# Sink tables on other engines, an output between two units, and two gate halves ahead of their val halves in a fused attention and SwiGLU kernel

## The chip, the cores and the metric

The kernel runs on one core of one Trainium2 chip. The metric is the device time of one execution in microseconds (us); for the kernel before the change four executions are given, and their median is 241.62 us. A change of 1% is 2.42 us. In the profile PE is TensorE's matmuls and PEld its weight loads, DVE is VectorE, ACT is ScalarE, POOL is GpSimd, SP is SyncE.

## What is computed

Windowed attention with four sink keys, then a SwiGLU block on its output (cut):

```python
# q, k, v: (4, 8, 768, 64); n_sink 4, window 128; x: 3072 tokens of 512
scores = scale * np.matmul(q, k.transpose(0, 1, 3, 2))
is_sink = pos[None, :] < int(n_sink)
rel = pos[:, None] - pos[None, :]
in_window = (rel >= 0) & (rel < int(window))
scores = np.where(is_sink | in_window, scores, -1000000000.0)
a = np.exp(scores - np.max(scores, axis=-1, keepdims=True))
a = a / (np.sum(a, axis=-1, keepdims=True) + 1e-09)
x = np.matmul(a, v).transpose(0, 2, 1, 3).reshape(B * S, H * D)
g = x @ w_gate                       # 512 x 1536
silu = g * (1.0 / (1.0 + np.exp(-g)))
val = x @ w_val                      # 512 x 1536
out = silu * val @ w_out             # 1536 x 512
```

## The kernel before

Everything is one hand-written order: each engine gets its instructions in the order in which the code issues them, and semaphores join the engines.

The 3072 tokens are cut in two ways. Attention works on 12 groups of 256 tokens (three for each of the four batches). The SwiGLU block works on eight token blocks of 256, 256, 256, 512, 512, 512, 512 and 256 tokens; block 0 is group 0, block 1 is group 1, block 2 is group 2, block 3 is groups 3 and 4, and so on.

For a group, `step_T` or `step_TN` transposes keys and queries on TensorE, or `xbar` lets SP's DMA queue do it from the tile `nat`. `step_S` makes the scores, ACT takes their exponential into `e`, and DVE multiplies by the window mask (L313). `step_K` multiplies the queries with the batch's sink keys, which `step_ks` has copied into `kss` (L274). `step_PV` starts from the sink values, which `step_vsb` has spread into the block-diagonal table `vsb` (L279), adds the window values, and then normalises into `xn`: DVE takes the reciprocal (L372) and either DVE multiplies (L378, put off until the next `flush`) or, with `norm="a"`, ACT does (L375). `step_X` turns `xn` into `xT`, the input of the block: by TensorE transposes for groups 0, 1, 2 and 4 (L402, evicted by ACT at L405 or by DVE at L409), by a DMA transpose on SP's queue for the others (L397).

A block is worked in units. A gate unit (`gate`) projects 512 columns with `w_gate` into the PSUM bank `pg` (eight matmuls of 256 columns, or four of 512), ACT takes `th`, then come the attention steps that are woven into the unit, then the projection with `w_val` into `pv`; DVE makes `u` from `th` and `pg` (L445) and `ht` from `u` and `pv` (L446). A down unit (`down`) multiplies `ht` with `w_out` for 128 tokens into `pd` (L463), ACT copies it out, and SP's queue issues the output DMA (L471). `weave` runs a list of units, each with the attention steps of its slot. The units of the first list are gate units 0, 1 and 2 of block 0 (columns f=0, 2, 4), then 0, 1 and 2 of block 1, then the rest of both; `wg`, `wv` come in six pieces of two column chunks, and unit f=4 needs the third piece, `wg2` and `wv2`. Both halves of a unit use PSUM banks from one ring of eight.

POOL issues all loads of q, k, v and the weights in one order. The order ends, before the first matmuls, with `load_nat(2)`, `load_gate(3)`, `load_v(2)`, `load_gate(4)`, `load_gate(5)` and the four pieces of `w_out`. There are eight semaphores for these loads, used in turn, so that a load waits until the eighth before it has landed. `nat` from group 4 on has one buffer: a load of the next group waits for the transposes of the last.

Of the kernel before, what the change touches and what calls it, by code (L numbers as in the profile page):

```python
# [7 lines left out]
FP32 = mybir.dt.float32  # L8
BF16 = mybir.dt.bfloat16
AF = mybir.ActivationFunctionType  # L10
ALU = mybir.AluOpType
# [3 lines left out]
def kernel(  # L15
# [12 lines left out]
    nc = tc.nc  # L28
    P = 128
# [7 lines left out]
    DMC = DM // P  # L37
# [4 lines left out]
    SIZES = [256, 256, 256, 512, 512, 512, 512, 256]  # L42
# [6 lines left out]
    FOF = [(i, f - sum(FCH[:i])) for i in range(len(FCH))  # L49
           for f in range(sum(FCH[:i]), sum(FCH[:i + 1]))]  # L50
# [27 lines left out]
    def bank(shape, dtype, name):  # L78
        return psum.tile(shape, dtype, tag="b", name=name)
# [24 lines left out]
    def load_nat(g):  # L104
        b, c = divmod(g, GC)
        x = (natp if g > 3 else rowp).tile(
            [P, 2, 2, DM], BF16, tag="nat" if g > 3 else "rows", name="nat")
        for i, src in ((0, k), (1, q)):
            for j in range(2):
                t0 = c * 256 + j * P  # L110
                nc.gpsimd.dma_start(  # L111
                    x[:, i, j].rearrange("p (h d) -> p h d", d=D),
                    src[b, :, t0:t0 + P].rearrange("h p d -> p h d"))
        nats[g] = x

    def load_v(g):
        b, c = divmod(g, GC)
        va = vpool.tile([P, 2, H, VS], BF16, tag=f"va{g}", name="va")
        nc.vector.memset(va[:, :, :, D:D + 1], 1.0)
        for j in range(2):  # L120
            t0 = c * 256 + j * P
            nc.gpsimd.dma_start(  # L122
                va[:, j, :, 0:D], v[b, :, t0:t0 + P].rearrange("h p d -> p h d"))
        vas[g] = va

    wgs, wvs, wos = [], [], []

    def load_gate(i, which=(0, 1)):
        f0, n = sum(FCH[:i]) * P, FCH[i] * P
        both = (wgs, moe_w_gate, "wg"), (wvs, moe_w_val, "wv")  # L130
        for lst, w, nm in (both[x] for x in which):
            t = wpool.tile([P, DMC, n], BF16, tag=f"{nm}{i}", name=nm)
            nc.gpsimd.dma_start(
                t, w[:, f0:f0 + n].rearrange("(c p) f -> p c f", p=P))
            lst.append(t)

    def load_out(i):
        n = DFC // 4
        t = wpool.tile([P, n, DM], BF16, tag=f"wo{i}", name="wo")
        nc.gpsimd.dma_start(  # L140
            t, moe_w_out[i * n * P:(i + 1) * n * P].rearrange("(c p) f -> p c f", p=P))
        wos.append(t)
# [57 lines left out]
    load_gate(1, (1,))  # L200
    load_gate(2)
    nc.gpsimd.tensor_copy(out=vcf[64:128], in_=vcf[0:64])
    load_nat(2)
    load_gate(3)
    load_v(2)
    load_gate(4)
    load_gate(5)
    for i in range(4):
        load_out(i)

    nc.vector.tensor_scalar(ident, tq, tk, None, op0=ALU.is_equal)
    tq2 = tq.rearrange("p (o x) -> p o x", o=1).broadcast_to([P, 2, P])
# [3 lines left out]
    kTs, qTs, es_t, e_t, xns, xTs = {}, {}, {}, {}, {}, {}  # L216
    later = []

    def flush():
        for f in later:  # L220
            f()
        later.clear()

    def new_T(b):
        if b not in kTs:
            kTs[b] = kqtp.tile([P, NP2, S], BF16, tag="kT", name="kT")
            qTs[b] = kqtp.tile([P, NP2, S], BF16, tag="qT", name="qT")

    def step_T(g, i, p2, evict=None):
        b, c = divmod(g, GC)  # L230
        new_T(b)
        x = rows[g]
        pt = bank([P, 2, 256], FP32, "pt")
        for pp in range(2):
            p = 2 * p2 + pp
            for r in range(4):
                for w in range(2):
                    h = slice(64 * w, 64 * (w + 1))
                    nc.tensor.matmul(
                        pt[h, pp, r:256:4], x[h, i, p, r * D:(r + 1) * D],  # L240
                        ident[h, h], start=True, stop=True, skip_group_check=True)
        dst = (kTs, qTs)[i][b][:, 2 * p2:2 * p2 + 2, c * 256:(c + 1) * 256]
        if (evict or ("a", "v")[i]) == "a":
            nc.scalar.copy(out=dst, in_=pt)
        else:
            nc.vector.tensor_copy(out=dst, in_=pt)
# [24 lines left out]
    def step_ks(b):  # L271
        for h in range(2):
            r = slice(h * D, (h + 1) * D)
            nc.vector.tensor_copy(  # L274
                out=kss[r, b, :, h * NS:(h + 1) * NS], in_=kTs[b][r, :, 0:NS])

    def step_vsb(b):
        vsb = const.tile([P, 4, D + 1], BF16, tag=f"vsb{b}", name="vsb")
        nc.vector.tensor_tensor(  # L279
            vsb,  # L280
            (vcl[:, b - 1:b] if b else vcf).broadcast_to([P, 4, D + 1]),
            diag_h.rearrange("q (h o) -> q h o", o=1).broadcast_to([P, 4, D + 1]),
            op=ALU.mult)
        vsbs.append(vsb)
# [100 lines left out]
    def dense(t, c, n):  # L385
        return t[:, 0:c * n].rearrange("p (c n) -> p c n", c=c)
# [27 lines left out]

    hts = {}

    def gate(tb, f, attn):
        n = SIZES[tb]
        two = 512 // n
        if tb not in hts:  # L420
            t = hpool.tile([P, DFC * 512], BF16, tag="ht", name="ht")
            hts[tb] = dense(t, DFC, n)
            if tb == 0:
                hts[1] = t[:, DFC * n:2 * DFC * n].rearrange("p (c n) -> p c n", c=DFC)
        x = xTs[tb]

        def project(ws, name):
            ps = bank([P, 512], FP32, name)
            for i in range(two):
                fi, fo = FOF[f + i]  # L430
                for c in range(DMC):
                    nc.tensor.matmul(  # L432
                        ps[:, i * n:(i + 1) * n], ws[fi][:, c, fo * P:(fo + 1) * P],
                        x[:, c], start=(c == 0), stop=(c == DMC - 1))
            return ps

        pg = project(wgs, "pg")
        th = tpool.tile([P, 512], FP32, tag="th", name="th")
        nc.scalar.activation(th, pg, AF.Tanh, scale=0.5)  # L439
        for a in attn:  # L440
            a()
        pv = project(wvs, "pv")

        u = upool.tile([P, 512], BF16, tag="u", name="u")
        nc.vector.scalar_tensor_tensor(u, th, 1.0, pg, op0=ALU.add, op1=ALU.mult)  # L445
        nc.vector.tensor_tensor(  # L446
            hts[tb][:, f:f + two].rearrange("p a n -> p (a n)"), u, pv, op=ALU.mult)
        flush()

    def down(tb, ts, attn, last=False):  # L450
# [26 lines left out]
    def gates(tb):  # L477
        return [(gate, tb, f) for f in range(0, DFC, 512 // SIZES[tb])]
# [4 lines left out]
    def A(fn, *a):  # L483
        return lambda: fn(*a)

    def TN(g, evict="av"):
        return [A(step_TN, g, i, j, evict) for j in range(2) for i in range(2)]

    def Ss(g):
        return [A(step_S, g, p2) for p2 in range(2)]  # L490

    def PVs(g):
        return [A(step_PV, g, j, hh) for hh in range(2) for j in range(2)]

    def Xs(g):
        return [A(step_X, g, j) for j in range(2)]

    def K(g):
        return A(step_K, g)
# [84 lines left out]
    for p in range(1, NP2):  # L584
# [2 lines left out]
    nc.vector.scalar_tensor_tensor(lt8, th8, 0.0, lt8, op0=ALU.is_ge, op1=ALU.mult)  # L587
    nc.vector.tensor_reduce(diag_h, lt8.rearrange("p q h -> p h q"), mybir.AxisListType.X,
                            op=ALU.max)
    step_T(1, 0, 0, "a")  # L590
    step_T(1, 0, 1, "a")
    step_T(1, 1, 0, "a")
    step_T(1, 1, 1, "a")
    for j in range(2):
        for hh in range(2):
            step_PV(0, j, hh)
# [4 lines left out]
    step_X(0, 0)  # L601
    step_X(0, 1)
    flush()
    step_ks(0)
    step_vsb(0)
    step_S(1, 1)
    later[:0] = masks1
    flush()
# [4 lines left out]
    load_sinks(vcl, 1, B)  # L613

    g0, g1, g2 = gates(0), gates(1), gates(2)
    us = [g0[0], g0[1], g0[2], g1[0], g1[1],
          g1[2], g0[3], g1[3], g0[4], g1[4], g0[5], g1[5],
          *g2, *downs(0), *downs(1), *downs(2)]

# [6 lines left out]
    def NV(g):  # L626
# [1 line left out]

    weave(us, slots(
        (0, [K(1)]), (1, PVs(1)[:2] + [A(step_PV, 1, 0, 1, "a"), A(step_PV, 1, 1, 1, "a"), flush]),  # L630
        (2, [A(step_X, 1, 0, "a"), A(step_X, 1, 1, "a")]),
        ((4, 4, 5, 5), TN(2)), ((6, 7), Ss(2)), (6, [K(2)]),
        ((8, 8), PVs(2)[:2]), (9, [A(step_PV, 2, 0, 1, "a"), A(step_PV, 2, 1, 1, "a")]),
        ((10, 11), [A(step_X, 2, 0, "a"), A(step_X, 2, 1, "a")]),
# [8 lines left out]
    def pair(ga, gb, sh=0):  # L643
        s = sh
        return [((s, s + 2), Ss(ga)), (s, [K(ga)]),
                ((s + 4, s + 5, s + 6, s + 7), PVs(ga)),
                ((s + 6, s + 8), Ss(gb)), ((s + 8, s + 9), Xs(ga)), (s + 6, [K(gb)]),
                ((12, 12, 13, 13) if s else (10, 11, 12, 13), PVs(gb)),
                ((14, 14) if s else (13, 14), Xs(gb))]

    weave(gates(3) + downs(3), slots(
        (2, [A(xbar, 7)]), (2, [NV(8)]),
        (5, [A(step_ks, 2), A(step_vsb, 2)]), *pair(5, 6),
        (15, [A(xbar, 8)]), (15, [NV(9)])))
    weave(gates(4) + downs(4), slots(
        *pair(7, 8), (3, [A(xbar, 9)]), (9, [A(step_ks, 3), A(step_vsb, 3)]),
        (3, [NV(10)]), (15, [A(xbar, 10)]), (15, [NV(11)])))
    weave(gates(5) + downs(5), slots(*pair(9, 10), (6, [A(xbar, 11)])))
    us = gates(6) + gates(7) + downs(6) + downs(7)
# [38 lines left out]
```

## Time and profile before

| what | value |
|---|---|
| four executions | 240.94, 241.51, 241.74, 243.13 us; median 241.62 us |
| the profiled execution | 243.13 us, of which the span is 241.3 us |
| PE busy | 229.8 us (95% of the span) |
| DVE busy | 158.8 us (66%) |
| ACT busy | 114.8 us (48%) |
| POOL busy | 73.8 us (31%) |
| PE L432 pg and pv, 753 matmuls | 147.1 us |
| PE L463 pd, 291 matmuls | 65.0 us |
| DVE L445 u and L446 ht, 72 each | 49.1 and 49.5 us |
| DVE L274 kss, 8 copies | 0.25 us median, 0.16 to 0.59 us |
| DVE L279 vsb, 4 products of 128x260 | 0.43 us each |

A group of instructions is read as: line, engine and operation, output and inputs by the names in the code, and count; then busy time, the mean of one in ns, and how long the engine stood idle before them and what ended most of that. The timeline gives start, duration, engine, line and operation, and in brackets the idle time ahead of the instruction with what released it. PE's busy time is an upper reading, since matmuls overlap and their ends are modelled.

The granted TensorE clock is 1.0 over the whole span.

### The profile page before, as it was taken

Reading aid. Unit: us, or ns where it says so; the run is one execution under the profiler, and the core shown is the slowest. Engines: PE = TensorE matmul, PEld = TensorE weight load, DVE = VectorE, ACT = ScalarE, POOL = GpSimd, SP = SyncE. Lnnn points to the kernel's source line nnn. Section 1 sums busy time; section 2 is a strip of 40 time slices with the busy share of each in tenths; the row PEclk is TensorE's granted clock in tenths of the full one; section 3 lists DMA queues with packets and bytes.
Section 4 is the critical chain, followed back from the end, with each engine's and each line's share of the span. In section 5 each row is a group of like instructions: output and inputs, shape, how many; then the busy total and the mean of one; then the engine's idle time right before and its main releaser. Section 6 shows DMA issues by size and latency. Waiting matters only on the chain.

```text
span 241.3 us, 4989 instructions
## 1 busy us (share of the span) xinstructions
PE 229.8 (95%) x1925; PEld 132.0 (55%) x1949; DVE 158.8 (66%) x337; ACT 114.8 (48%) x236; POOL 73.8 (31%) x97
## 2 busy tenths in 40 slices
PE   7898999999996998999999999999999999999994
PEld 4566978895553444454445444445454445488443
DVE  4797778768661698970597991388981498877100
ACT  4886485467441655511656602556512662232111
POOL 8985865703507026080080800053000000000000
PEclk9999999999999999999999999999999999999999
DMA  8999999993999999999599994679604200200132
GB/s 140 161 181 176 182 201 202 154 129 66 146 109 162 212 110 123 142 84 201 111 105 157 88 88 130 102 103 144 93 0 130 90 0 0 46 0 3 45 130 87
DMA packets 107655, 27.36 MB, mean 113 GB/s; under 512 B 94704, under 2 KB 104688, under 8 KB 107632
## 3 DMA queue, kind: packets, MB, share of 16 engines
q0 software_dynamic: 76640, 13.90, 73.9%
q1 hardware_dynamic: 30448, 12.89, 26.9%
q8 instruction: 15, 0.25, 0.4%
q10 hardware_dynamic: 544, 0.26, 0.4%
q14 instruction: 8, 0.07, 0.1%
HBM read 28.34 MB, written 6.29 MB: 144 GB/s over the span
## 4 chain that ended last, share of the span: by engine, by line
PE 83%; DMA 8%; DVE 3%; issue 2%; POOL 2%; ACT 1%; SPq 0%; POOLq 0%; DVEq 0%; ACTq 0%
PE pd L463 24%; PE pv L432 24%; PE pg L432 24%; DMA wv<-in_moe_w_val_dram 4%; PE o L364 4%; PE s L301 4%; DMA rows<-in_q_dram 2%; DMA xT<-xn 2%; PE pn L254 1%; POOL rows L100 1%; POOL x L188 1%; DVE ht L446 1%; PE pk L329 1%; PE o L344 1%; DVE xn L378 1%
## 5 line engine op out<-in xcount | busy, mean ns | idle before, releaser
L432 PE MATMUL pg<-xT,wg 128*128 128x256 bf16 (+1 forms) x377 | 73.5, 325 | 3.0 <-DMA xT<-xn 1.8
L432 PE MATMUL pv<-xT,wv 128*128 128x256 bf16 (+1 forms) x376 | 73.6, 325 | 1.5 <-DMA wv<-in_moe_w_val_dram 0.7
L439 ACT ACTIVATE th<-pg 128x512 f32<-128x512 f32 x72 | 43.4, 603 | 65.3 <-PE pg L432 61.4
L445 DVE SCALAR_TENSOR_TENSOR u<-th,pg 128x512 bf16<-128x512 f32 x72 | 49.1, 682 | 38.1 <-ACT th L439 38.1
L463 PE MATMUL pd<-wo,ht 128*128 128x512 bf16 (+2 forms) x291 | 65.0, 370 | 0.4
L446 DVE TENSOR_TENSOR ht<-u,pv 128x512 bf16<-128x512 bf16 x72 | 49.5, 687 | 12.0 <-PE pv L432 5.2
L432 PEld LDWEIGHTS <-wg 128*128 128x128 bf16 x384 | 37.3, 98 | 28.7 <-issue 3.5
L432 PEld LDWEIGHTS <-wv 128*128 128x128 bf16 x384 | 34.3, 98 | 20.8 <-issue 1.7
L308 ACT ACTIVATE e<-s 128x512 bf16<-128x512 f32 (+1 forms) x88 | 42.8, 582 | 4.3 <-PE s L301 4.3
L463 PEld LDWEIGHTS <-ht 128*128 128x128 bf16 x300 | 27.7, 98 | 29.2 <-issue 0.5
L111 POOL DMA_DIRECT2D nat<-in_k_dram x20 | 17.6, 884 | 81.2 <-DMA qT<-nat 78.2
L468 ACT ACTIVATE ot<-pd 128x512 f32<-128x512 f32 (+1 forms) x24 | 14.3, 596 | 48.1 <-PE pd L463 46.2
L313 DVE TENSOR_TENSOR e<-e,mask 128x1024 bf16<-128x1024 bf16 (+1 forms) x44 | 26.9, 649 | 3.6 <-ACT e L308 3.6
L122 POOL DMA_DIRECT2D va<-in_v_dram x24 | 21.5, 918 | 5.0 <-DMA wo<-in_moe_w_out_dram 2.5
L364 PEld LDWEIGHTS <-e 128*128 128x128 bf16 x352 | 15.4, 98 | 8.2 <-issue 0.2
L378 DVE TENSOR_TENSOR xn<-o,rcp 128x256 bf16<-128x256 f32 x44 | 18.7, 424 | 1.5
L111 POOL DMA_DIRECT2D nat<-in_q_dram x20 | 17.7, 897 | 1.2 <-DMA wg<-in_moe_w_gate_dram 0.5
L364 PE MATMUL o<-va,e 128*128 128x65 bf16 x352 | 17.5, 193 | 0.2
L301 PE MATMUL s<-qT,kT 64*128 64x128 bf16 (+1 forms) x240 | 13.1, 237 | 0.5 <-DVE ht L446 0.5
L301 PEld LDWEIGHTS <-kT 64*128 64x128 bf16 x240 | 7.7, 94 | 7.9 <-issue 7.3
L372 DVE RECIPROCAL rcp<-o 128x4 f32<-128x4 f32 x48 | 8.1, 174 | 5.4 <-PE o L364 5.4
L470 DVE TENSOR_SCALAR ot<-pd 128x128 f32<-128x128 f32 x1 | 0.3, 292 | 14.3 <-PE pd L463 14.3
(71 smaller groups left out, 87.5 us busy)
## 6 DMA issues: line engine op xcount, KB each, us to landing
out_dram<-ot SPq DMA_DIRECT2D x23, 256.0 KB
va<-in_v_dram POOLq DMA_DIRECT2D x24, 128.0 KB, 6.2
nat<-in_k_dram POOLq DMA_DIRECT2D x20, 128.0 KB, 4.3
nat<-in_q_dram POOLq DMA_DIRECT2D x20, 128.0 KB, 6.1
wg<-in_moe_w_gate_dram POOLq DMA_DIRECT2D x6, 256.0 KB, 8.0
wv<-in_moe_w_val_dram POOLq DMA_DIRECT2D x6, 256.0 KB, 8.5
wo<-in_moe_w_out_dram POOLq DMA_DIRECT2D x4, 384.0 KB, 11.1
st<-in_q_dram ACTq DMA_DIRECT2D x2, 128.0 KB
```

The costliest lines, as they stand in the source:

```text
L111: nc.gpsimd.dma_start(x[:, i, j].rearrange("p (h d) -> p h d", d=D), src[b, :, t0:t0 + P].rearrange("h p d -> p h d"))
L122: nc.gpsimd.dma_start(va[:, j, :, 0:D], v[b, :, t0:t0 + P].rearrange("h p d -> p h d"))
L301: nc.tensor.matmul(pss[2 * pp + h][:, col:col + n], kTs[b][r, p, kk:kk + P], qTs[b][r, p, qq:qq + n], start=True, stop=True)
L308: nc.scalar.activation(e_t[g][:, h0 + h, lo:512], pss[2 * pp + h][:, lo:512], AF.Exp, scale=scale)
L313: nc.vector.tensor_tensor(e, e, m[:, :, lo:512].broadcast_to([P, 2, 512 - lo]), op=ALU.mult)
L364: nc.tensor.matmul(o, l, r, start=(c == 0 and i == 0), stop=(i == len(mms) - 1), skip_group_check=True)
L378: nc.vector.tensor_tensor(xn, po[:, :, 0:D], rcp.broadcast_to([P, 4, D]), op=ALU.mult)
L432: nc.tensor.matmul(ps[:, i * n:(i + 1) * n], ws[fi][:, c, fo * P:(fo + 1) * P], x[:, c], start=(c == 0), stop=(c == DMC - 1))
L439: nc.scalar.activation(th, pg, AF.Tanh, scale=0.5)
L445: nc.vector.scalar_tensor_tensor(u, th, 1.0, pg, op0=ALU.add, op1=ALU.mult)
L446: nc.vector.tensor_tensor(hts[tb][:, f:f + two].rearrange("p a n -> p (a n)"), u, pv, op=ALU.mult)
L463: nc.tensor.matmul(po, hts[tb][:, f, ts * P:(ts + 1) * P], wos[f // n][:, f % n, lo:hi], start=(f == 0), stop=(f == DFC - 1))
```

## The change

Four things change.

1. For batch 0, `step_ks` runs on ACT (`nc.scalar.copy`) and `step_vsb` on POOL; for batches 1 to 3 both stay on DVE. `step_ks(0)` is issued after the four `step_T` of group 1, before `step_PV` of group 0 (it stood behind `step_X` of group 0). `step_vsb(0)` is issued after the reduction that makes `diag_h`, and the tail of the load order (`load_nat(2)` to `load_out`) is issued behind it. On POOL's queue the loads have the same order as before, with the one product ahead of `load_nat(2)`.
2. `step_X` of group 1, which stood inside unit f=4 of block 0 between its gate half and its val half, is issued as a unit of its own between the second and the third unit (`alone`, a function that was there but unused: it runs its steps and then `flush`). The second of its two transposes is evicted by DVE at once ("now") and no longer by ACT.
3. Unit f=4 of block 0 and unit f=0 of block 1 are issued together (`both`): both gate halves, then both val halves.
4. `step_ks` and `step_vsb` of batch 2 move from gate unit 5 of block 3 to its last down unit (slot 15), and those of batch 3 from gate unit 9 of block 4 to its last down unit. This stands in the diff, and not in the few words of the title.

```diff
@@ loads
-    load_nat(2)
-    load_gate(3)
-    load_v(2)
-    load_gate(4)
-    load_gate(5)
-    for i in range(4):
-        load_out(i)
...
@@ step_ks, step_vsb
-            nc.vector.tensor_copy(
+            (nc.vector.tensor_copy if b else nc.scalar.copy)(
                 out=kss[r, b, :, h * NS:(h + 1) * NS], in_=kTs[b][r, :, 0:NS])
...
-        nc.vector.tensor_tensor(
+        (nc.vector if b else nc.gpsimd).tensor_tensor(
             vsb,
...
@@ gate
+    def gate_a(tb, f):
...
+        pg = project(wgs, tb, f, "pg")
         th = tpool.tile([P, 512], FP32, tag="th", name="th")
         nc.scalar.activation(th, pg, AF.Tanh, scale=0.5)
+        return pg, th
+
+    def gate_b(tb, f, pg, th):
+        pv = project(wvs, tb, f, "pv")
         u = upool.tile([P, 512], BF16, tag="u", name="u")
         nc.vector.scalar_tensor_tensor(u, th, 1.0, pg, op0=ALU.add, op1=ALU.mult)
...
+    def gate(tb, f, attn):
+        a = gate_a(tb, f)
+        for step in attn:
+            step()
+        gate_b(tb, f, *a)
+        flush()
+
+    def both(one_, two_, attn):
+
+        a = [gate_a(*x) for x in (one_, two_)]
+        for x, y in zip((one_, two_), a):
+            gate_b(*x, *y)
         flush()
...
@@ the start
+    step_vsb(0)
+    load_nat(2)
+    load_gate(3)
+    load_v(2)
+    load_gate(4)
+    load_gate(5)
+    for i in range(4):
+        load_out(i)
     step_T(1, 0, 0, "a")
     step_T(1, 0, 1, "a")
     step_T(1, 1, 0, "a")
     step_T(1, 1, 1, "a")
+    step_ks(0)
...
     step_X(0, 0)
     step_X(0, 1)
     flush()
-    step_ks(0)
-    step_vsb(0)
     step_S(1, 1)
...
-    us = [g0[0], g0[1], g0[2], g1[0], g1[1],
+    us = [g0[0], g0[1], (alone, 0, 0), (both, g0[2][1:], g1[0][1:]), g1[1],
           g1[2], g0[3], g1[3], g0[4], g1[4], g0[5], g1[5],
...
-        (2, [A(step_X, 1, 0, "a"), A(step_X, 1, 1, "a")]),
+        (2, [A(step_X, 1, 0, "a"), A(step_X, 1, 1, "now")]),
...
@@ blocks 3 and 4
-        (5, [A(step_ks, 2), A(step_vsb, 2)]), *pair(5, 6),
+        (15, [A(step_ks, 2), A(step_vsb, 2)]), *pair(5, 6),
...
-        *pair(7, 8), (3, [A(xbar, 9)]), (9, [A(step_ks, 3), A(step_vsb, 3)]),
+        *pair(7, 8), (3, [A(xbar, 9)]), (15, [A(step_ks, 3), A(step_vsb, 3)]),
```

More of the change, by code (lines that the diff above doesn't have):

```diff
@@ L415, with project @@
     hts = {}
-    def gate(tb, f, attn):
+    def project(ws, tb, f, name):
         n = SIZES[tb]
-        two = 512 // n
+        ps = bank([P, 512], FP32, name)
+        for i in range(512 // n):
+            fi, fo = FOF[f + i]
+            for c in range(DMC):
+                nc.tensor.matmul(
+                    ps[:, i * n:(i + 1) * n], ws[fi][:, c, fo * P:(fo + 1) * P],
+                    xTs[tb][:, c], start=(c == 0), stop=(c == DMC - 1))
+        return ps
+    def gate_a(tb, f):
+        n = SIZES[tb]
         if tb not in hts:
@@ L424, in gate @@
                 hts[1] = t[:, DFC * n:2 * DFC * n].rearrange("p (c n) -> p c n", c=DFC)
[L425 to L437, printed above, removed]
+        pg = project(wgs, tb, f, "pg")
         th = tpool.tile([P, 512], FP32, tag="th", name="th")
         nc.scalar.activation(th, pg, AF.Tanh, scale=0.5)
-        for a in attn:
-            a()
-        pv = project(wvs, "pv")
+        return pg, th
+    def gate_b(tb, f, pg, th):
+        pv = project(wvs, tb, f, "pv")
         u = upool.tile([P, 512], BF16, tag="u", name="u")
@@ L446, in gate @@
         nc.vector.tensor_tensor(
-            hts[tb][:, f:f + two].rearrange("p a n -> p (a n)"), u, pv, op=ALU.mult)
+            hts[tb][:, f:f + 512 // SIZES[tb]].rearrange("p a n -> p (a n)"), u, pv,
+            op=ALU.mult)
+    def gate(tb, f, attn):
[8 more added lines that the diff above has]
+            gate_b(*x, *y)
         flush()
```

## The prediction

> **What bounds the kernel now.** I read the page's slices and chain first, then PE's idle stretches, then the timeline around each.
>
> ```profile
> PEclk9999999999999999999999999999999999999999
> DMA  8999999993999999999599994679604200200132
> PE 83%; DMA 8%; DVE 3%; issue 2%; POOL 2%; ACT 1%; SPq 0%; POOLq 0%; DVEq 0%; ACTq 0%
> ```
>
> PE holds 83% of the chain at full clock, so the change can gain only what PE waits. Behind the start-up (up to 5 us) the matmul records show idle stretches of 0.30 us at 20.65, 0.70 at 22.44, 1.80 at 76.54, 0.51 at 92.69, 0.23 at 93.52 and 0.37 at 139.53, and about 1.5 us more in pieces of 0.1 to 0.35. The DMA row says that the engines are full up to 54 us and again from 60 to 115.
>
> The timeline around the moved units:
>
> ```profile
> 20.94 1.05 PE L432 MATMUL pg<-xT,wg 128*128 128x256 bf16 x8 [0.30 <-DVE xn L378]
> 21.83 0.61 PE L402 MATMUL px<-ident,xn 128*128 128x128 bf16 x8
> 23.13 1.05 PE L432 MATMUL pv<-xT,wv 128*128 128x256 bf16 x8 [0.69 <-DMA wv<-in_moe_w_val_dram]
> 25.76 0.49 PE L432 MATMUL pg<-xT,wg 128*128 128x256 bf16 x3
> ```
>
> The third unit's val half waits for `wv2`, which lands at 23.1; unit f=2 of block 1 starts at 25.76. Further on, SP's queue and the chain:
>
> ```profile
> 67.60 1.64 SPq L268 DMA_TRANSPOSE qT<-nat  x1
> 69.33 1.22 SPq L268 DMA_TRANSPOSE kT<-nat  x1
> 70.64 1.22 SPq L268 DMA_TRANSPOSE qT<-nat  x1
> 71.95 0.53 SPq L471 DMA_DIRECT2D out_dram<-ot  x1
> 72.58 2.53 SPq L397 DMA_TRANSPOSE xT<-xn  x2
> 73.90 4.30 DMA xT<-xn
> 78.33 0.81 PE pg L432 x3
> ```
>
> Block 3 starts at 78.33 on a transfer that SP issued at 73.90, at the end of an unbroken row of issues from 67.60, when a `nat` load landed. SP's waits name it: 4.9 us on `nat` q loads, 4.5 of it at once. POOL issued that load at 60.01, 8.47 us late, on the transposes of the `nat` before. Those waited for loads that POOL issued from 42.04 to 44.82 on `w_out` landings. So this stall is the end of a row of transfers that goes back into the full DMA stretch; PE's gate units are not in it.
>
> DVE in block 3, gate units 5 and 6, and in block 4, unit 9:
>
> ```profile
> 90.43 0.52 DVE L274 COPY kss<-kT 64x16 bf16<-64x16 bf16 x2
> 90.95 0.43 DVE L279 TENSOR_TENSOR vsb<-vcl,diag_h 128x260 bf16<-128x260 f32 x1
> 91.30 0.68 DVE L445 SCALAR_TENSOR_TENSOR u<-th,pg 128x512 bf16<-128x512 f32 x1
> 92.46 0.69 DVE L446 TENSOR_TENSOR ht<-u,pv 128x512 bf16<-128x512 bf16 x1 [0.48 <-PE pg L432]
> 93.20 0.32 PE L301 MATMUL s<-qT,kT 64*128 64x256 bf16 x3 [0.51 <-DVE ht L446]
> 93.76 1.04 PE L432 MATMUL pv<-xT,wv 128*128 128x512 bf16 x4 [0.23 <-DVE xn L378]
> ...
> 138.82 0.43 DVE L279 TENSOR_TENSOR vsb<-vcl,diag_h 128x260 bf16<-128x260 f32 x1
> 139.16 0.68 DVE L445 SCALAR_TENSOR_TENSOR u<-th,pg 128x512 bf16<-128x512 f32 x1
> 139.90 1.02 PE L432 MATMUL pg<-xT,wg 128*128 128x512 bf16 x4 [0.37 <-DVE u L445]
> ```
>
> Both times the tables stand in front of a `u` whose `th` is ready, and PE then waits for DVE to free a bank.
>
> **Batch 0's tables.** DVE loses 0.55 (kss) and 0.43 (vsb) at 14.86 to 15.87. The masks behind them can start at 14.95 and no longer 15.79, but the last needs ACT's eighth exponential, which ends at 17.08; so the last mask ends near 17.8 where it ended at 18.28. PE does not wait for it: the sink matmuls at 18.13 stand behind PE's own pg, and the val half at 19.60 behind `wv1`. Worth on PE: 0; DVE runs 0.3 to 0.5 earlier.
> ACT gets two copies of 64x16. No such row on ACT: its 64-element rows take 0.22 (1.74 over 8), DVE's same copies up to 0.59, so 0.44 to 1.18; I take 0.44, the row of the same engine. ACT is idle for 0.80 just there, before the exponentials at 13.05. At 1.18 the exponentials slip by 0.4, and PE loses up to 0.4 ahead of 19.60.
> POOL gets a 128x260 product. POOL's rows are copies of 65 elements in 0.23 and of 195 in 0.34; the slope gives 0.40 for 260 with one input, the short copy four times and doubled for two inputs 1.84. I take 0.8, the slope's value doubled. It runs from 14.2, behind the `vcf` copy; queued behind it are the loads `nat(2)`, `wg3`, `wv3` and the rest. `nat(2)`'s first issue moves from 14.37 to 15.2, the next from 15.80 to 16.1, the last of its four from 17.7 to about 18, `wg3` from 18.54 to 18.8; `wv3` is held to 19.84 by its own wait on `wv1`, so the delay ends there. Each transfer has a backlog ahead of it (`wv2`, issued at 13.02, lands at 23.1), so no landing moves. The sinks need `vsb` at 18.13: cost 0, even at 1.84; it would show only above 3.9 us.
> The Trainium skill speaks against this move: GPSIMD Engine Reference, section 4.1 Engine selection, puts elementwise products on VectorE and calls GpSimd about twice as slow with two inputs. By that rule and DVE's 0.43 the product takes 0.86 as an estimate, and the sum below stays as it is.
>
> **`step_X` alone, and the two gate halves.** PE is free at 20.5, after unit f=2's val half. The first transposes find `xn` ready; the second wait for ACT's `xn`, eight instructions from 19.81 to 21.55 (before, the gate half lay over this wait). They end at 21.9; pg of f=4 runs to 22.8 (0.87 per eight matmuls). DVE ends `ht` at 22.30 and evicts in 0.42 by 22.75, so block 1's pg starts at 22.8, and the val halves follow at 23.7 and 24.6 without waiting for `wv2`. Unit f=2 of block 1 starts near 25.4: 0.3 gained, up to 0.6 with DVE's head start, down to a loss of 0.4 if the DVE eviction is late.
> What is late next is the stall at 76.54. If its transfers keep their times, PE waits 0.3 longer there. I count 0; bounds 0 and 0.6. A loss in front is hidden by the same 1.8 us.
>
> **Tables of batch 2.** Without 0.87 us of tables `u` starts at 90.8, when `th` (90.14 and 0.60) is there: 0.50 earlier. The 0.48 ahead of `ht` is not explained: val matmuls ended by 91.2. If it stays, PE gets back 0.50 of its 0.74 of waits; if it goes, all 0.74. I take 0.6; the lower bound is 0, should that wait be PE's own. Next late is only PE's matmuls.
>
> **Tables of batch 3.** `u` moves from 139.16 to 138.8, its bank is free at 139.5, when PE asks: 0.37 gained, all of it.
>
> **Where the tables go.** In the last down units DVE stands idle (7.68 us before its `u` at 116.83), which hides some 1.0 us of tables; the first sink matmul that needs them is at 116.64. Without that idle time it would cost that 1.0. SP's and POOL's order does not change there.
>
> Sum: 0 + 0 + 0.6 + 0.37, about 1.0. The profiled execution: span 241.3 less 1.0 is 240.3, with 1.83 around it 242.1. It was 1.51 above the median, so a median of 240.6.
>
> **Rivals.**
> *The stall before block 3 shrinks too.* The first output leaves SP at 60.12, when ACT has it; PE earlier by 0.3 would send it into the slices before 60, where DMA is a third busy, and clear the way for the `nat` loads. For: the `nat` q load took over 7 us beside that output. Against: the row hangs on loads. Worth up to the stall, 1.8, and the front's 0.35: down to 238.5.
> *DVE's time comes back.* The tables only uncover the 0.48 wait or another mask: nothing kept, 241.2 to 242.1.
> *Slower: the output goes ahead of the `nat` loads.* The same output, 0.3 earlier, now enters the queues before the `nat` q load issued at 60.01 and holds it by up to half of that output's 3.7 us to landing. SP's unbroken row and block 3 move by 1.8; less the 1.0 behind, 242.4. It decides once that q load lands more than 1.0 later than 67.6, past 68.6.
> *The change doesn't do what it says* can be set aside in part: the instructions are where it says, but "off VectorE" is worth nothing on PE, by the first step.
>
> **How the numbers follow.** As summed: 0.46, between 240.1 and 241.2. The stall shrinks: 0.26, 238.5 to 240.1. Nothing kept: 0.16, 241.2 to 242.1. Slower: 0.12, 242.1 to 244.5, with the unseen in it. The four runs before differ from their median by -0.7 to +1.5, so I leave some half a us to a median of runs. The range is 238.6 to 242.4: it leaves out the far end of the first rival and most of the last case. Faster or slower by over 1%, 2.42 us, is what a measurement here can tell from no change. Below 239.2 lies a good half of the first rival, 0.15, and 0.07 of larger gains in it that I don't see: 0.22. Above 244.0 I put 0.10, nearly all of the last case, for what the trace doesn't show. Within 1%: 0.68.
>
> **What would show it.** Right: the two val halves of `both` run without a wait on `wv`; PE's idle time before block 3 is longer by 0.3; no idle time before PE's scores of group 6 (92.7) or at 139.5; ACT's two copies lie in an idle stretch before the exponentials; POOL's product under 2 us. Wrong: PE idle over 1 us before the second transposes of group 1; `ht` after `u` in unit 5 still late; a first `pg` of block 3 that moves by over 1 us in either direction; `pk` of group 7 waiting for `kss`.

## The result, and the profile after

| | before | after the change |
|---|---|---|
| median | 241.36 us (56 runs) | 241.18 us (35 runs) |
| range | 240.42 to 243.13 us | 239.24 to 244.0 us |
| profiled execution, span | 243.13, 241.3 us | 241.74, 239.9 us |

Compared with the runs of the kernel before that were made beside it, the changed kernel takes 0.9974 of the time, 95% interval 0.9961 to 0.9986: 0.26%, some 0.6 us, faster. That is within 1%, inside the range, and less than the 1.0 us of the sum. The two longest of the 35 runs, 243.06 and 244.0 us, ran at a granted clock of 0.993 and are left out of this ratio.

The page's slices and chain of the changed kernel, for the lines shown first of the kernel before:

```profile
PEclk9999999999999999999999999999999999999999
DMA  8999999993999999999599994899504200200132
PE 85%; DVE 5%; DMA 4%; ACT 2%; issue 2%; POOL 1%; SPq 0%; POOLq 0%; DVEq 0%; ACTq 0%
```

The DMA share of the chain has halved, from 8% to 4%: the waits on `wv` are gone from it, and its share of `xT<-xn` has gone from 2% to 4%. The clock is the same, and the shape of the DMA row nearly so.

The timeline of the changed kernel at the start (start, duration, engine, line, operation, idle time ahead and its releaser):

```profile
12.21 0.45 ACT L267 COPY kss<-kT 64x16 bf16<-64x16 bf16 x2
...
13.00 4.05 ACT L301 ACTIVATE e<-s 128x512 bf16<-128x512 f32 x8 [0.35 <-PE s L294]
...
14.25 0.62 POOL L272 TENSOR_TENSOR vsb<-vcf,diag_h 128x260 bf16<-128x260 f32 x1
...
14.82 1.84 POOL L111 DMA_DIRECT2D nat<-in_k_dram  x2
...
18.43 0.77 POOL L133 DMA_DIRECT2D wg<-in_moe_w_gate_dram  x1
...
20.46 1.24 PE L395 MATMUL px<-ident,xn 128*128 128x128 bf16 x8
...
21.53 1.04 PE L416 MATMUL pg<-xT,wg 128*128 128x256 bf16 x8
...
22.73 1.05 PE L416 MATMUL pg<-xT,wg 128*128 128x256 bf16 x8 [0.16 <-DVE xT L402]
...
23.61 1.91 PE L416 MATMUL pv<-xT,wv 128*128 128x256 bf16 x16
...
25.36 1.04 PE L416 MATMUL pg<-xT,wg 128*128 128x256 bf16 x8
```

ACT's copies lie in its idle time; the exponentials start at 13.00, where they started at 13.05. The POOL product takes 0.62 us, and `wg3` leaves at 18.43, not later than the 18.54 before. The two val halves are one row of 16 matmuls without a wait on `wv2`, and unit f=2 of block 1 starts at 25.36 instead of 25.76.

SP's queue and PE ahead of block 3, in two views of the same profile:

```profile
66.28 1.19 SPq L261 DMA_TRANSPOSE qT<-nat  x1
67.56 1.77 SPq L261 DMA_TRANSPOSE kT<-nat  x1
69.42 1.22 SPq L261 DMA_TRANSPOSE qT<-nat  x1
70.74 0.54 SPq L476 DMA_DIRECT2D out_dram<-ot  x1
71.38 2.53 SPq L390 DMA_TRANSPOSE xT<-xn  x2
```

```profile
72.73 3.40 PE L468 MATMUL pd<-wo,ht 128*128 128x512 bf16 x14
77.13 1.02 PE L416 MATMUL pg<-xT,wg 128*128 128x512 bf16 x4 [1.01 <-DMA xT<-xn]
```

The same unbroken row of issues, here 1.3 us earlier, and a wait of 1.01 where 1.80 stood. So the `nat` q load did not land past 68.6, which the slower rival of the prediction needs. Then the tables of batches 2 and 3, block 3 first:

```profile
89.56 0.69 DVE L436 SCALAR_TENSOR_TENSOR u<-th,pg 128x512 bf16<-128x512 f32 x1 [0.25 <-ACT th L430]
...
90.35 0.69 DVE L437 TENSOR_TENSOR ht<-u,pv 128x512 bf16<-128x512 bf16 x1
...
91.04 0.50 PE L294 MATMUL s<-qT,kT 64*128 64x256 bf16 x8
...
91.65 1.04 PE L416 MATMUL pv<-xT,wv 128*128 128x512 bf16 x4
```

`u` now waits for `th` alone, `ht` follows it, and the scores of group 6 are one row without a break. In block 4 the matmuls that waited 0.37 for `u` at 139.90 follow their predecessors at once:

```profile
137.62 1.02 PE L416 MATMUL pv<-xT,wv 128*128 128x512 bf16 x3
138.48 1.03 PE L416 MATMUL pg<-xT,wg 128*128 128x512 bf16 x4
```

But ahead of block 4 there is a wait that was not there (the chain):

```profile
108.67 0.34 SPq L476
109.01 0.45 issue
109.46 0.02 SPq L390
109.48 0.06 issue
109.54 4.68 DMA xT<-xn
114.22 0.04 issue
114.26 1.02 PE pg L416 x4
```

The second transfer of group 6's output lands 4.68 us after its issue, 1.06 us after PE has run out of work. Before the change the same transfer was issued at 111.66 and block 4 started at 115.14, without a wait. POOL's first loads for group 8, before and after, and before the change the transfer and block 4:

```profile
102.77 1.76 POOL L111 DMA_DIRECT2D nat<-in_k_dram  x2 [8.50 <-DMA qT<-nat]
102.08 1.76 POOL L111 DMA_DIRECT2D nat<-in_k_dram  x2 [8.70 <-DMA qT<-nat]
...
111.66 1.20 SPq L397 DMA_TRANSPOSE xT<-xn  x1
115.14 1.03 PE L432 MATMUL pg<-xT,wg 128*128 128x512 bf16 x4
```

The starts of the blocks (the first pg matmul of each, from the PE timelines) add up to the difference of the two profiled spans:

| | block 3 | to block 4 | to block 5 | to block 6 | to the end |
|---|---|---|---|---|---|
| before | 78.33 | 36.81 | 37.57 | 35.77 | 52.8 |
| after | 77.13 | 37.13 | 37.04 | 35.78 | 52.8 |
| difference | -1.20 | +0.32 | -0.53 | +0.01 | 0 |

### The profile page after: what moved, and what is told of

Read it like the earlier page. It is cut to its first block, busy times and chain, and to the rows that moved or that the text cites. A ratio compares the mean times of both kernels' runs of the same rounds, so it can differ in the third digit from the quotient of the medians.

```text
span 239.9 us, 4986 instructions
## 1 busy us (share of the span) xinstructions
PE 230.0 (96%) x1925; PEld 132.6 (55%) x1949; DVE 158.8 (66%) x335; ACT 114.5 (48%) x237; POOL 74.5 (31%) x98
## 4 chain that ended last, share of the span: by engine, by line
PE 85%; DVE 5%; DMA 4%; ACT 2%; issue 2%; POOL 1%; SPq 0%; POOLq 0%; DVEq 0%; ACTq 0%
PE pv L416 26%; PE pg L416 25%; PE pd L468 22%; PE o L357 4%; PE s L294 4%; DMA xT<-xn 4%; DVE xn L371 1%; PE pn L247 1%; PE o L337 1%; PE pt L544 1%; POOL x L188 1%; PE pk L322 1%; ACT e L565 1%; ACT th L430 1%; DVE u L436 1%
```

## The experiments

My theory: the tables of batches 2 and 3 carry the gain, and what the start gains is eaten by the transfers ahead of block 3. Rivals: the start carries it; or the transfers carry it. All ratios are to the kernel before, from five rounds.

**The parts, one at a time.**

Without the last part:

```diff
-        (15, [A(step_ks, 2), A(step_vsb, 2)]), *pair(5, 6),
+        (5, [A(step_ks, 2), A(step_vsb, 2)]), *pair(5, 6),
...
-        *pair(7, 8), (3, [A(xbar, 9)]), (15, [A(step_ks, 3), A(step_vsb, 3)]),
+        *pair(7, 8), (3, [A(xbar, 9)]), (9, [A(step_ks, 3), A(step_vsb, 3)]),
```

> The change without its last part: the tables of batches 2 and 3 stand again in gate unit 5 of block 3 and unit 9 of block 4. Theory (the gain comes from those tables; what the start gains is eaten by the transfer before block 3): ratio to the kernel before 0.999 to 1.001, 241.1 to 241.6 us; unit f=2 of block 1 starts near 25.4 as after the change; the waits of 0.5 and 0.2 us behind unit 5 of block 3 and of 0.37 in block 4 are back. Rival (the start is worth its 0.4 us to the end): 0.997 to 0.998, as the whole change.

Measured: 0.9988 (0.9967 to 1.001). Unit f=2 of block 1 starts at 24.88; behind unit 5 of block 3 PE idles 0.21 and 0.24, in block 4 0.39. A gain can't be told from none, which fits the theory; the interval does not exclude the rival's 0.997 either.

Only the last part, put into the kernel before (the same diff backwards):

> The kernel before, with the tables of batches 2 and 3 moved to the last down units and nothing else. Theory: ratio 0.996 to 0.998, 240.4 to 240.9 us, all that the whole change gains; from the first pg of block 3 to the val half of its unit 6 it takes 14.5 us, where it took 15.4; a wait for xT stands before block 4. Rival (the start counts): 0.999 to 1.001.

Measured: 0.9946 (0.9925 to 0.9967), 239.83 us, from six runs. A wait stands ahead of block 4, but a short one:

```profile
112.36 1.02 PE L432 MATMUL pg<-xT,wg 128*128 128x512 bf16 x4 [0.31 <-DMA xT<-xn]
```

From the first pg of block 3 to the val half of its unit 6 it takes 14.53 us, as expected. The tables alone gain. The ratio is below the whole change's 0.9974, but the two intervals overlap (0.9961 to 0.9967).

Only the two moves of units:

```diff
+    us = [g0[0], g0[1], (alone, 0, 0), (both, g0[2][1:], g1[0][1:]), g1[1],
...
+        (2, [A(step_X, 1, 0, "a"), A(step_X, 1, 1, "now")]),
```

> The kernel before, with the output of group 1 as a unit of its own and the two gate halves ahead of the val halves, all tables where they were. Theory: the val half of f=4 no longer waits for wv2, unit f=2 of block 1 starts 0.2 to 0.4 us earlier than at 25.76, and the time is that of before: 0.999 to 1.001. Rival (the units alone carry the change): 0.997 to 0.998. Rival (the two moves need each other): without DVE's free time the second eviction is late, unit f=2 of block 1 starts after 25.8, ratio 1.000 to 1.002.

Measured: 0.9986 (0.9966 to 1.0006); unit f=2 of block 1 starts at 25.05. The rival that the moves need DVE's free time falls. The rival that the units alone carry the change (0.997 to 0.998) lies inside the interval and is not excluded.

Only batch 0's tables on ACT and POOL, with the tail of the load order behind the product:

```diff
+            (nc.vector.tensor_copy if b else nc.scalar.copy)(
...
+        (nc.vector if b else nc.gpsimd).tensor_tensor(
```

> The kernel before, with batch 0's tables on ACT and POOL (and the tail of the load order behind the product on POOL) and nothing else. Theory: DVE is earlier by some 0.4 us at 17 to 19 us and PE is not, since wv1, wg2 and wv2 set its waits: unit f=2 of block 1 at 25.7 to 25.8, ratio 0.999 to 1.001. Rival (VectorE held the start): unit f=2 of block 1 earlier by over 0.3 us, ratio 0.998.

Measured: 0.9997 (0.9975 to 1.0019). The PE timeline at the start:

```profile
20.02 1.05 PE L416 MATMUL pv<-xT,wv 128*128 128x256 bf16 x8 [0.36 <-DMA wv<-in_moe_w_val_dram]
21.40 1.05 PE L416 MATMUL pg<-xT,wg 128*128 128x256 bf16 x8 [0.34 <-DMA wg<-in_moe_w_gate_dram]
...
25.84 0.93 PE L416 MATMUL pg<-xT,wg 128*128 128x256 bf16 x7
```

PE waits for weights, as the theory said, and no gain can be told from none.

**The transfers.** The changed kernel with two buffers for `nat`:

```diff
-    natp = pool("natp", 1)
+    natp = pool("natp", 2)
```

> The changed kernel, with two buffers instead of one for the nat tiles of groups 4 to 11, so that a load no longer waits for the transposes of the group before it. Theory (the waits before block 3 and block 4, 1.01 and 1.06 us in the changed kernel's profile, are the end of a row load, transposes, load, transposes): both waits under 0.3 us, ratio to the kernel before 0.990 to 0.995. Rival (the DMA engines are full, and loads that run ahead only delay outputs and transposes): a wait of over 1 us stays at one of the two places, or a new one comes, ratio 0.996 to 1.002.

Measured: 0.996 (0.9945 to 0.9974). Both waits are gone, and a new one comes where group 4's scores need their transposed queries:

```profile
62.26 0.56 PE L294 MATMUL s<-qT,kT 64*128 64x256 bf16 x10 [0.78 <-DMA qT<-nat]
```

Both theories hold by half: the two waits do come from the single buffer, and a new wait of under 1 us stands at another transpose. That the loads that run ahead cause it is the rival's reading; no run tests it. Group 8's loads now leave POOL from 87.21, and group 6's second transfer lands 2.54 us after its issue:

```profile
109.15 1.20 SPq L390 DMA_TRANSPOSE xT<-xn  x1
112.65 1.03 PE L416 MATMUL pg<-xT,wg 128*128 128x512 bf16 x4
```

Against the whole change's 0.9974 the gain is not clear of the intervals.

Group 3's output by TensorE:

```diff
-    PEX = (0, 1, 2, 4)
+    PEX = (0, 1, 2, 3, 4)
```

> The changed kernel, with group 3's output transposed by TensorE and evicted by DVE instead of by SP's queue. Group 4's already is, so block 3 then waits for no transfer. PE pays eight more transposes, about 0.9 us. Theory: the wait before block 3 (0 to 1.8 us in the profiles so far, mean 0.9) is gone and the time stays about the same as the changed kernel's: ratio to the kernel before 0.995 to 0.999; the wait before block 4 stays or grows. Rival (PE's work alone sets the end): 0.9 us more than the changed kernel, 1.000 to 1.003.

Measured: 0.9957 (0.9942 to 0.9972); no wait ahead of block 3 or 4 in its profile. The transposes cost no time that can be seen; that the wait ahead of block 4 would stay was wrong. Here group 8's loads leave at 99.69, 2.4 us before those of the changed kernel, and group 6's second transfer lands at 110.99, 1.0 us before block 4 starts. That they leave earlier because SP's queue has two transfers less is likely, and not shown.

The kernel before with the tables moved and two buffers:

> The kernel before, with the tables of batches 2 and 3 in the last down units and two nat buffers, without the change of the start. Theory: as the changed kernel with two buffers, but the start's 0.4 us now missing, since no transfer is left to eat it: ratio 0.991 to 0.996, 0.2 to 0.6 us behind that kernel. Rival (the start's change is worth nothing or costs): equal to it or ahead of it.

Measured: 0.9937 (0.9915 to 0.9959), the lowest ratio of all, with an interval that overlaps those of the tables alone and of the changed kernel with two buffers; the new wait at the scores is 0.81 here. It is not behind the changed kernel with two buffers, so the rival stands.

The changed kernel once more:

> The changed kernel once more, beside the others on one chip. Theory: ratio 0.996 to 0.999, with a wait at the start of block 3 or of block 4 that differs from the 1.01 and 1.06 us of its first profile by up to 1 us, since the landings of the nat loads scatter; the waits behind unit 5 of block 3 (0.51 and 0.23) and in block 4 (0.37) stay gone. Rival (the wait of 1.06 us before block 4 belongs to the change): within 0.2 us of 1.06 again.

Measured: 0.9975 (0.9956 to 0.9994). Its twelve runs lie in two heaps, seven from 239.16 to 240.23 and five from 241.14 to 241.6. The profiled one is of the upper heap, and its wait ahead of block 4 is longer still:

```profile
114.17 1.02 PE L416 MATMUL pg<-xT,wg 128*128 128x512 bf16 x4 [1.58 <-DMA xT<-xn]
```

It waits 0.41 ahead of block 3.

The tables alone, a second time:

> The kernel before with only the tables of batches 2 and 3 moved, a second time. In every profile with these tables moved the gates of block 4 take 37.04 us to block 5 (37.5 to 37.6 otherwise), so theory: ratio 0.994 to 0.997 again, block 4 to block 5 in 37.04. Rival (the 0.9946 of its first runs, six of them, was the scatter of the transfers): 0.997 to 0.999, as the whole change.

Measured: 0.9946 (0.9926 to 0.9965) from twelve runs, block 4 to block 5 in 37.04, waits of 0.41 and 0.36 ahead of blocks 3 and 4. The rival that the first 0.9946 was scatter falls.

The changed kernel with group 6's output by TensorE (`PEX = (0, 1, 2, 4, 6)`):

> The changed kernel, with group 6's output transposed by TensorE and evicted by DVE instead of by SP's queue. Theory (the wait of 1.06 and 1.58 us before block 4 is the second transfer of group 6, landing behind group 8's loads): block 4 then starts without a wait, PE does 0.9 us more there, the median moves by less than 0.5 us from the changed kernel's: ratio to the kernel before 0.995 to 0.998, and the spread of the runs shrinks. Rival (something else holds block 4, such as group 5's transfers): a wait of 0.5 us or more stays before block 4.

Measured: 0.9964 (0.9942 to 0.9987). Block 4 starts without a wait:

```profile
112.41 1.03 PE L416 MATMUL pg<-xT,wg 128*128 128x512 bf16 x4
```

So it is group 6's transfer. The spread did not shrink, 239.69 to 241.7, so this wait is not what spreads the runs; and 0.9964 is not clear of the changed kernel's 0.9974.

The v loads ahead of the `nat` loads, first in the changed kernel, then in the kernel with the tables alone:

```diff
-        return L(A(load_nat, g), A(load_v, g))
+        return L(A(load_v, g), A(load_nat, g))
```

> The changed kernel, with each group's two v loads issued ahead of its four nat loads and no longer behind them, for groups 4 to 11. The v loads wait for no transposes, so they leave earlier. Theory (in the wait before block 4 group 6's output lands right after the v loads of group 8): the wait before block 4 is under 0.3 us, that before block 3 under 0.5 us, ratio to the kernel before 0.992 to 0.996. Rival (the v loads now lie in front of the nat loads and hold the row): the waits stay or grow, 0.997 to 1.002.

> The kernel before with the tables of batches 2 and 3 moved and the v loads ahead of the nat loads, the start as before the change. Theory: no wait before block 3 or 4 over 0.3 us, ratio 0.993 to 0.997, and behind the changed kernel with the same loads by the start's 0.4 us. Rival (the start is worth nothing to the end): within 0.1 us of it, or ahead.

Measured: 0.9975 (0.9952 to 0.9998) and 0.999 (0.9966 to 1.0013). Ahead of block 3 neither idles, ahead of block 4 they idle 1.25 and 0.68; the first:

```profile
113.16 1.02 PE L416 MATMUL pg<-xT,wg 128*128 128x512 bf16 x4 [1.25 <-DMA xT<-xn]
```

The theory falls: it is not the v loads in particular that group 6's transfer lands behind. They have landed by 97.52 and 97.26 here, and the waits stand all the same.

## Why the prediction was right, step by step

The stretches between block starts tell the steps apart, since they don't depend on when block 3 starts. The profiles of the parts, and of one kernel without a wait ahead of block 4 to compare with:

| kernel | block 3 to 4 | PE idle ahead of 4 | block 4 to 5 |
|---|---|---|---|
| before | 36.81 | none | 37.57 |
| without the last part | 36.65 | none | 37.59 |
| units only | 36.40 | none | 37.46 |
| batch 0's tables only | 36.65 | none | 37.61 |
| after | 37.13 | 1.06 | 37.04 |
| after, again | 37.64 | 1.58 | 37.04 |
| tables 2 and 3 only | 36.38 | 0.31 | 37.04 |
| the same, again | 36.43 | 0.36 | 37.04 |
| after, two buffers | 35.90 | none | 37.04 |

**Batch 0's tables: worth 0, and no worth was measured (0.9997).** ACT's copies took 0.45 for an estimated 0.44. POOL's product took 0.62 for an estimated 0.8, within 0.40 and 1.84, against 0.43 on DVE: 1.44 times. So the Trainium skill (GPSIMD Engine Reference, section 4.1 Engine selection), which says about twice for two inputs, is right in the direction for so small a product; the estimate of 0.86 worked out from it was too much. The last mask ends at 17.78, predicted 17.8.

**The two moves of units: 0.3 at unit f=2 of block 1, right.** Over the profiles that unit starts at 25.12 in the mean of eight with the new start and 25.51 of six with the old: 0.39. One profile would not have shown it, for the old start alone scatters from 25.25 to 25.84.

**The stall ahead of block 3: the step as worded was wrong, its worth is open.** I said that PE would wait 0.3 longer if the transfers kept their times. They don't keep them, and the prediction's own sign of being wrong, a first `pg` of block 3 that moves by over 1 us, came true: it moved by 1.20. With one `nat` buffer, group 3 on SP's queue and the loads in their old order, block 3 starts at 76.06, 76.25, 76.44, 76.53 and 77.13 with the new start and at 75.98, 76.43, 77.84 and 78.33 with the old. The 1.80 of the profile before was the worst of all. That the start is worth nothing at the end, which I counted, is neither shown nor refuted: the intervals of 0.9988 and 0.9986 hold 1, and also 0.9984, which 0.39 us kept whole would give. So it is open too whether the transfers eat it.

**The tables of batch 2: predicted 0.6; 0.69.** Block 3 without a wait behind it takes 35.90 with the tables moved. With them it takes 36.81, 36.49, 36.40 and 36.65, mean 36.59 (of the kernel without the last part, 0.16 are taken off: by the count of the next step its block 4 waited so long). The 0.48 ahead of `ht` that I could not explain went along with the tables in the changed kernel; its cause is still open.

**The tables of batch 3: predicted 0.37; 0.42 to 0.57, mean 0.52.** The idle time in the records is too short as a price. A row of eight pv matmuls is shown as 1.05 us and the next row starts 0.87 after it, so a modelled end lies some 0.17 behind the point at which the next matmul could have started. A wait costs its idle time and 0.17: 0.37 is 0.54, the wait of 1.06 ahead of block 4 is 37.13 less 35.90, 1.23, and that of 1.58 is 1.74. The 0.51 and 0.23 of batch 2 add up to 0.74, and with one such overlap to the 0.91 by which block 3 of the first profile was longer than 35.90; why one and not two fits there is not shown.

**What is late next: wrong, and the loss that the sum lacks.** For batch 2 I wrote "Next late is only PE's matmuls". Next late was group 6's transfer: it gave back 1.23 and 1.74 us in the two profiles of the changed kernel and 0.48 and 0.53 with the tables alone. Before the change it landed at 114.40, 0.7 ahead of block 4, and the prediction does not name it. Its issue moves with PE; the loads that are in flight beside it move far less. POOL's loads for group 8 moved from 102.77 to 102.08 and block 3 ended 2 us earlier; the transfer took 2.7 us from issue to landing before, and 4.7.

In all eleven profiles with one `nat` buffer and this transfer on SP's queue, it lands 11.3 to 12.4 us after group 8's first load leaves POOL, though its own issue lies anywhere from 7.2 to 8.9 us after that load. So what PE gains in block 3 moves the issue and hardly the landing. With two buffers the loads leave some 22 us before the transfer and it takes 2.5 us.

So 0.69 and 0.52 were gained, 1.21 together and more than the 0.97 of the sum. The two profiled executions of the changed kernel lost all of it again; both are long ones of their kernel (241.74 with a median of 241.18, and 241.6 with 240.21). That the 0.6 us of the ratio are what is left on average, some half, is worked out and not traced in a short execution. So that the sum came near is partly luck: its terms were too small, and it had no term for the loss. That the wait is this transfer's is shown by the change of `PEX` for group 6 and by the two buffers; in the first, block 3 takes 36.35 us, which is 0.45 over the 35.90, for the transposes that TensorE then does. That the wait accounts for the whole difference in the times is not shown.

The prediction took 1% for the least change that can be told from none; the intervals here are some 0.13% to either side for the change.

**Open.** The tables alone gave 0.9946 twice, the whole change 0.9974 and 0.9975; the intervals overlap a little. The transfer ahead of block 4 lands at 114.2 and 114.1 in the whole change and at 112.3 and 112.8 in the tables alone, while block 3 starts at 77.13 and 76.53, and at 75.98 and 76.43. Group 8's first load leaves at 102.08 and 101.70 against 100.40 and 100.62, so the landing follows the loads; these wait for the transposes of the group before. Why that row is later in the whole change is not shown. The kernel before with the last part alone and a second `nat` buffer has the lowest ratio, 0.9937: barely clear of the whole change's 0.9974 (0.9959 against 0.9961 at the ends of the intervals), and not of the tables alone.

## What to carry to other kernels

Take each moved piece back by itself before believing in the headline: here the part that the few words did not name is the only one whose gain alone stands clear of the noise. A slack in front of a transfer is a slack only against what moves with it; ask of each transfer whether the loads beside it follow the engine that gets faster. And when a wait is priced from idle time between modelled ends, see how far two matmul rows overlap elsewhere in the same profile: here 0.17 us had to be added to each wait ahead of a block.

## What the hardware showed

The DMA transpose of group 6's second 128 rows took 2.7 us from issue to landing in the kernel before, 3.9 with the tables alone, and 4.7 and 5.2 in two profiles of the changed kernel, with the loads of one group in flight beside it; with two `nat` buffers, and none of these loads in flight, 2.5. The times of the changed kernel fell in two heaps about 1 us apart in one series on one chip (seven runs to 240.23, five from 241.14, none between), so one profile shows only one of the outcomes. What makes the heaps is not shown.
